# Attention and softplus MLP in split fp32: fewer round trips of the weights through DRAM, a new order of instructions

## The chip, the cores and the metric

The kernel runs on one core of a Trainium2 chip. The metric is the device time of one execution in microseconds, the median of several runs. The engines are TensorE (PE, matmuls; PEld is its weight load), VectorE (DVE), ScalarE (ACT), GpSimd (POOL, hardly used here) and SyncE (SP), which in this kernel issues the DMA transfers.

## The reference

A batch of attention with 32 states per head, 8 batches, 8 heads, 512 tokens, head width 64, is read in both directions, and the rows of both reads go through one MLP with a softplus:

```python
scores = scale * x @ state.T;  a = softmax(scores);   xread = a @ state
scores2 = scale * state @ x.T; a2 = softmax(scores2); sread = a2 @ x
y = concatenate([xread, sread])     # 8 x (512 + 32) rows per head
rows = y.transpose(0, 2, 1, 3).reshape(4352, 512)
out = softplus(rows @ w_in) @ w_out    # 512 -> 2048 -> 512
```

All inputs and the output are fp32 in value.

## The kernel before

**Arithmetic.** TensorE works in fp32r. A value is held as a high part, cast to fp32r, and a low part, the rest. ScalarE makes the high part (`copy`, L302), VectorE the low part by a subtraction (L318); the helper `split` (L314) makes both. A product then takes three passes (high by high, high by low, low by high). Each of the sixteen 128-row tiles of w_out is so split into a tile `W` of 128x1024 words, 512 KB; w_in is kept as eight 512 KB tiles `wf` of two 512-wide halves, and each half is split into a tile `u`, sixteen of 512 KB.

**Stages.** Batches 0 and 1, then 2, go through `gemm2` (L605): hidden tile `h`, softplus `t` (L589), split into `g`, and `acc` sums `W` times `g` over the sixteen tiles. From batch 3 on, pairs of hidden tiles and pairs of w_out tiles are multiplied in a form with seven products of half size (L762; the first half of batch 3 still plain, L772). The forms of w_out that this needs are made by VectorE and ScalarE between batch 2 and batch 3 from tiles `Wc`: sums `ci` (L690), the differences `cf` (L696 to L699), and their splits `T`, `E`, `W` (names F, E and Wc in the trace). The rows of the second read, `sread`, come from all batches and are calculated as an extra batch "8" between batches 6 and 7; their w_in tiles are `uu`. A read of states is `R` in the plan (`rp` in the trace); it takes the turned softmax weights `aT`, which go from VectorE's transposes to DRAM (`te`) and back in pieces. K products (`vq`, from `u` and `K`) make the folded weights `vt` of batches 4 to 7, stored as `vd` and loaded as `V`.

**What goes through DRAM.** Each `W` is stored once (`Sw`, `wd<-W`) and loaded again as `Wb` (tiles 8 to 15, for batch 2) and as `Wc` (all sixteen, for batch 3 and later, `Lc`). Each `u` is stored (`Su`, `ud<-u`) and loaded at the sread rows as `uu` (`Lu`).

**Order.** A text `PLAN` at the head of the kernel lists all some 2,580 steps, each with its engine (T is TensorE, A ScalarE, V VectorE, S SP; a few conversions of the inputs have letters of their own) and the buffers its results take. Every engine runs its steps in the order of that text, and SP issues the transfers in that order too, each after what it reads is there and the buffer it writes is free. A buffer comes free with the last reader of what it held. So the text sets both the order and what can collide.

Of the kernel before, what the change touches and what calls it, by code (L numbers as in the profile page):

```python
# [8 lines left out]
F32 = mybir.dt.float32  # L9
# [9 lines left out]
P = 128  # L19
# [18 lines left out]
PAIRS = ("w8", "o8", "x", "xT", "po", "wf", "W", "V", "a", "g", "u", "K", "vt", "gA", "gS", "F", "ev", "uu", "Wb", "Wc", "E")  # L38
# [73 lines left out]
Sv.2.1.0:S: m.2.11.2:T: s.2.15:A:13 Sv.2.1.1:S: m.2.11.3:T: gh.2.15:A:31 B.K3.0+K3.1:T:7,2,0,4 ci1.0:V:12 uh.3.3:A:6 uh.3.2:A:39 ul.3.3:V: m.2.12.0:T:
gh.v3.0.0:A:20 ul.3.2:V: Su.3.3:S: gh.v3.0.1:A:24 m.2.12.1:T: gl.v3.0.0:V: Su.3.2:S: gh.v3.1.0:A:22 m.2.12.2:T: gl.v3.0.1:V: gh.v3.1.1:A:15
# [172 lines left out]
def graph(io, at, nc):  # L286
# [10 lines left out]
    def r(ap):  # L297
        return ap.bitcast(F32R)
# [295 lines left out]
    def which(f, b):  # L594
        return "W" if b < 2 or b == 2 and f < 8 else "Wb" if b == 2 else "Wc"
# [354 lines left out]
```

## Time and profile before

| | |
|---|---|
| median of 3 runs | 655.26 us (653.18 to 655.49) |
| the profiled execution | 654.07 us, of which the span from first to last instruction 651.9 |
| mean granted TensorE clock | 0.987 |
| busy: TensorE, VectorE, ScalarE | 622.6, 460.7, 369.1 us |
| moved by DMA | 124.25 MB, HBM read 76.81 and written 46.66 |

TensorE is the busiest engine. Where a row shows a time in brackets, that is how long the engine stood before the group of instructions, and what it then got. A DMA row on SP is the time of issuing; the data lands later.

### The profile page before, as it was taken

Reading aid. Unit: us, or ns where it says so; the run is one execution under the profiler, and the core shown is the slowest. Engines: PE = TensorE matmul, PEld = TensorE weight load, DVE = VectorE, ACT = ScalarE, POOL = GpSimd, SP = SyncE. Lnnn points to the kernel's source line nnn. Section 1 sums busy time; section 2 is a strip of 40 time slices with the busy share of each in tenths; the row PEclk is TensorE's granted clock in tenths of the full one; section 3 lists DMA queues with packets and bytes.
Section 4 is the critical chain, followed back from the end, with each engine's and each line's share of the span. In section 5 each row is a group of like instructions: output and inputs, shape, how many; then the busy total and the mean of one; then the engine's idle time right before and its main releaser. Section 6 shows DMA issues by size and latency. Waiting matters only on the chain.

```text
span 651.9 us, 11867 instructions
## 1 busy us (share of the span) xinstructions
PE 622.6 (95%) x4398; PEld 527.6 (81%) x4398; DVE 460.7 (71%) x1005; ACT 369.1 (57%) x743; POOL 1.0 (0%) x7
## 2 busy tenths in 40 slices
PE   8999999999839999989799999999999999999997
PEld 6678787776626787768688999989899999999997
DVE  4998595647715586859988698479874666745493
ACT  4989684754806575556545664376563435445540
POOL 0000000000000000000000000000000000000000
PEclk9999999999959999999899999999999999999999
DMA  8952332303987999998665143547358124723000
GB/s 340 418 194 98 116 122 76 120 33 109 387 347 319 382 355 395 417 417 294 191 199 131 50 136 108 184 137 214 98 185 275 59 98 163 227 76 87 1 33 33
DMA packets 49113, 124.25 MB, mean 191 GB/s; under 512 B 6816, under 2 KB 16544, under 8 KB 49056
## 3 DMA queue, kind: packets, MB, share of 16 engines
q1 hardware_dynamic: 48912, 122.97, 53.8%
q8 instruction: 35, 0.57, 0.4%
q10 hardware_dynamic: 144, 0.52, 0.2%
q14 instruction: 22, 0.18, 0.1%
HBM read 76.81 MB, written 46.66 MB: 189 GB/s over the span
## 4 chain that ended last, share of the span: by engine, by line
PE 77%; DVE 10%; DMA 7%; SPq 3%; issue 1%; ACT 1%; DVEq 0%; ACTq 0%
PE h L321 25%; PE acc L321 19%; PE pk_X L762 8%; PE pk_Z L762 7%; PE pk_Y L762 7%; PE pk_Q L762 4%; PE vp L321 2%; SPq L312 2%; PE vq L321 2%; DMA aT<-te 2%; DMA wd<-W 2%; DVE gA L318 1%; DMA Wc<-wd 1%; DMA out_dram<-o 1%; PE sc L321 1%
## 5 line engine op out<-in xcount | busy, mean ns | idle before, releaser
L321 PE MATMUL h<-a,V 128*128 128x512 f32 x744 | 180.7, 391 | 2.4 <-ACT t L734 2.4
L321 PEld LDWEIGHTS h<-a,V 128*128 128x128 f32 x744 | 137.4, 188 | 31.2 <-ACT t L734 2.8
L321 PE MATMUL acc<-W,g 128*128 128x512 f32 x480 | 118.8, 397 | 0.0
L321 PEld LDWEIGHTS acc<-W,g 128*128 128x128 f32 x480 | 89.7, 189 | 26.1 <-issue 6.3
L734 ACT ACTIVATE t<-h 128x256 f32<-128x256 f32 x152 | 50.2, 384 | 67.5 <-PE h L321 55.5
L302 ACT CAST gS<-sf 128x512 fp32r<-128x512 f32 x73 | 45.1, 622 | 42.9 <-DVE sf L746 13.6
L318 DVE TENSOR_TENSOR gA<-t,gA 128x384 fp32r<-128x384 f32 (+1 forms) x76 | 42.4, 560 | 28.8 <-ACT gA L302 28.5
L318 DVE TENSOR_TENSOR gS<-sf,gS 128x512 fp32r<-128x512 f32 x73 | 49.4, 682 | 9.8 <-ACT gS L302 7.6
L302 ACT CAST gA<-t 128x384 fp32r<-128x384 f32 (+1 forms) x76 | 39.0, 521 | 23.6 <-PE pk_Q L762 9.3
L762 PE MATMUL pk_X<-Wc,gA 128*128 128x256 f32 x240 | 43.3, 288 | 3.1 <-DVE rs L481 1.6
L744 DVE TENSOR_TENSOR sf<-t 128x256 f32<-128x256 f32 x66 | 27.5, 417 | 24.3 <-ACT t L734 24.2
L318 DVE TENSOR_TENSOR g<-t,g 128x512 fp32r<-128x512 f32 x48 | 32.2, 684 | 15.7 <-ACT g L302 15.7
L762 PEld LDWEIGHTS pk_X<-Wc,gA 128*128 128x128 f32 x240 | 36.8, 191 | 6.7 <-DVE gA L318 3.7
L762 PE MATMUL pk_Z<-Wc,gS 128*128 128x256 f32 x240 | 41.8, 283 | 0.0
L762 PE MATMUL pk_Z<-Wc,gA 128*128 128x256 f32 x240 | 41.8, 283 | 0.0
L762 PE MATMUL pk_Y<-F,gS 128*128 128x256 f32 x240 | 41.8, 283 | 0.0
L762 PE MATMUL pk_Y<-Wc,gS 128*128 128x256 f32 x240 | 41.8, 283 | 0.0
L762 PE MATMUL pk_Q<-E,gA 128*128 128x256 f32 x240 | 41.8, 283 | 0.0
L762 PE MATMUL pk_X<-F,gS 128*128 128x256 f32 x240 | 41.8, 283 | 0.0
L589 ACT ACTIVATE t<-h 128x512 f32<-128x512 f32 x48 | 27.7, 600 | 24.6 <-PE h L321 23.4
L762 PEld LDWEIGHTS pk_Z<-Wc,gA 128*128 128x128 f32 x240 | 34.6, 192 | 0.0
L762 PEld LDWEIGHTS pk_Q<-E,gA 128*128 128x128 f32 x240 | 34.6, 192 | 0.0
(167 smaller groups left out, 973.7 us busy)
## 6 DMA issues: line engine op xcount, KB each, us to landing
vd<-vt SPq DMA_DIRECT2D x32, 512.0 KB, 7.5
V<-vd SPq DMA_DIRECT2D x128, 128.0 KB, 3.1
w<-in_w_in_dram SPq DMA_DIRECT2D x16, 512.0 KB, 8.2
o<-in_w_out_dram SPq DMA_DIRECT2D x16, 512.0 KB, 9.8
x<-in_xn_dram SPq DMA_DIRECT2D x16, 512.0 KB, 4.8
wd<-W SPq DMA_DIRECT2D x16, 512.0 KB, 9.6
ud<-u SPq DMA_DIRECT2D x16, 512.0 KB, 6.4
Wc<-wd SPq DMA_DIRECT2D x16, 512.0 KB, 10.3
```

The costliest lines, as they stand in the source:

```text
L302: nc.scalar.copy(dst, src)
L312: op(name, "S", ins, list(outs), lambda e: nc.sync.dma_start(dst(), src()))
L318: lambda e: eng(e).tensor_tensor(r(dlo()), src(), dhi(), ALU.subtract))
L321: nc.tensor.matmul(dst, lhs, rhs, start=start, stop=stop)
L589: lambda e: nc.scalar.activation(at(f"t.{k}"), at(f"h.{k}"), AF.Softplus))
L734: nc.scalar.activation(dst, src.rearrange("p (c t) -> p c t", t=P), AF.Softplus)
L744: nc.vector.tensor_tensor(o[:, 0:2], a[:, 0:3:2], a[:, 3:4].broadcast_to([P, 2, P]), ALU.subtract)
L762: nc.tensor.matmul(at(bank)[:, 256 * half:256 * half + 256], r(g[:, gi, P * blk:P * blk + P]), r(wform(u, m)(wi)), start=first and pi == p ...
```

## The change

Three things are changed in the code.

- **W.** Only tiles 8 to 15 are stored (`Sw`), earlier and each near where its split is finished; they are loaded as `Wb` for batch 2 as before and as `Wc` for batch 3 and later. Tiles 0 to 7 keep their place on chip to the end: batch 3 and later read `W.0` to `W.7` in place of `Wc.0` to `Wc.7` (`which`, `wt`).
- **w_in for the sread rows.** The sixteen stores of `u` and loads of `uu` are replaced by eight stores of the unsplit `wf` (`Sf`, `fd<-wf`) and eight loads (`Lf`, into `wg`). `wg` is split anew by sixteen casts `xh` on ScalarE and sixteen subtractions `xl` on VectorE into `uu`.
- **A new `PLAN`** from there on: same matmuls, another order on all engines and other buffers.

```diff
+AWAY, BACK = (8, 9, 10, 11, 12, 13, 14, 15), (8, 9, 10, 11, 12, 13, 14, 15)
 PLAN = """
...
-Lx.1.0:S:0 Lx.1.1:S:2 qk.2.1:A:6 Sw.13:S: h.2.0:T:6 A.3.0:V:0 Sw.11:S: qk.3.1:A:2 Sw.10:S: qk.3.0:A:10 vl.2.1.0:V: Sw.1:S: o.0.2.2:V: Sw.9:S:
+tl.0:V: m.1.15.3:T: m.1.13.1:T: o.1.1.3:V: m.1.14.1:T: Ms.2.0:V: Sw.15:S: Sw.13:S: Sw.14:S: So.1.3:S: m.1.15.1:T: Se.1.0:S: m.1.12.2:T: o.1.1.1:V:
...
     def which(f, b):
-        return "W" if b < 2 or b == 2 and f < 8 else "Wb" if b == 2 else "Wc"
+        return "Wc" if b > 2 and f in BACK else "Wb" if b >= 2 and f in AWAY else "W"
 
-    for f in range(NFT):
+    for f in sorted({*AWAY, *BACK}):
         store(f"Sw.{f}", [f"W.{f}:h", f"W.{f}:l"], lambda f=f: io.wd[f], lambda f=f: at(f"W.{f}"), [f"D:wd.{f}"])
-        for w in ("Wb", "Wc")[f < 8:]:
+        for w in ["Wb"] * (f in AWAY) + ["Wc"] * (f in BACK):
             load(f"L{w[1]}.{f}", [f"{w}.{f}:h", f"{w}.{f}:l"], lambda f=f, w=w: at(f"{w}.{f}"), lambda f=f: io.wd[f], [f"D:wd.{f}"])
...
     for c in range(4):
+        for i in range(2):
+            whole = [W1[0, j, i] for j in range(2)] if c == 0 else [W1[c, 2 * i + q] for q in range(2)]
+            store(f"Sf.{c}.{i}", whole, lambda c=c, i=i: io.fd[c, i], lambda c=c, i=i: at(f"wf.{c}.{i}"), [f"D:fd.{c}.{i}"])
+            load(f"Lf.{c}.{i}", [f"wg.{c}.{i}:"], lambda c=c, i=i: at(f"wg.{c}.{i}"), lambda c=c, i=i: io.fd[c, i], [f"D:fd.{c}.{i}"])
         for q in range(4):
...
-            store(f"Su.{k}", [f"u.{k}:h", f"u.{k}:l"], lambda k=k: io.ud[k], lambda k=k: at(f"u.{k}"), [f"D:ud.{k}"])
-            load(f"Lu.{k}", [f"uu.{k}:"], lambda k=k: at(f"uu.{k}"), lambda k=k: io.ud[k], [f"D:ud.{k}"])
+            split(f"xh.{k}", f"xl.{k}", lambda c=c, q=q: page(f"wg.{c}.{q // 2}", 2, 512)[:, q % 2],
+                  lambda k=k: page(f"uu.{k}", 2, 512)[:, 0], lambda k=k: page(f"uu.{k}", 2, 512)[:, 1], [f"wg.{c}.{q // 2}:"], f"uu.{k}:h", f"uu.{k}:l", "A")
...
-            op(f"ci{i}.{u}", "V", [f"Wc.{f}:h", f"Wc.{f}:l"], [f"{buf}:0"],
+            op(f"ci{i}.{u}", "V", [f"{wt(f, 3)}:h", f"{wt(f, 3)}:l"], [f"{buf}:0"],
...
-            op(f"h.8.{u}.{i}", "T", [f"uu.{u // 2}.{kt}:" for kt in range(4)] + [f"sreadT:{x}{b}" for b in range(B) for x in "hl"],
+            op(f"h.8.{u}.{i}", "T", [f"uu.{u // 2}.{kt}:{x}" for kt in range(4) for x in "hl"] + [f"sreadT:{x}{b}" for b in range(B) for x in "hl"],
```

The same replacement of `Wc` by `wt(f, 3)` stands in the splits and products of the later batches. Three places of the new order follow.

SP, at the start of batch 2, before. `wd<-W` is a store `Sw`, `aT<-te` a piece of the turned softmax weights of the read of batch 1, x the rows it reads; the sixteen stores begin right after x.

```order
L309 DMA x_0_1718<-in_xn_dram 128x1024
L309 DMA x_1_1720<-in_xn_dram 128x1024
L312 DMA wd_111<-W_1444 128x1024
L312 DMA wd_109<-W_1079 128x1024
...
L312 DMA wd_102<-W_664 128x1024
L312 DMA out_dram<-po_1_498 128x512
L312 DMA te_70<-tr_0_1794 128x512
L309 DMA aT_0_1586<-te_68 32x4x128 x3
L312 DMA te_71<-tr_1_1815 128x512
L312 DMA te_73<-tr_1_1828 128x512
L309 DMA ks<-in_stk_dram 64x4x128
```

The same place of SP in the changed kernel:

```order
L313 DMA out_dram<-po_0_500 128x512
L310 DMA x_0_1726<-in_xn_dram 128x1024
L310 DMA x_1_1728<-in_xn_dram 128x1024
L310 DMA ks<-in_stk_dram 64x4x128 x2
L310 DMA aT_0_1594<-te_68 32x4x128 x3
L313 DMA te_70<-tr_0_1777 128x512
L313 DMA te_71<-tr_1_1779 128x512
L313 DMA out_dram<-po_1_490 128x512
L313 DMA out_dram<-po_0_500 128x512
L313 DMA te_73<-tr_1_1835 128x512
```

The pieces of `aT` stand behind x and ks, and no store of W is left there: seven of the eight stand before batch 1's outputs, one further ahead.

TensorE, around the read of batch 1, before. `vp` is a product for the folded weights of batch 3, `rp` the read, `acc` the sums of batch 2 with the hidden tile `g_1`, the second of the batch.

```order
L321 MATMUL vp_3_1_1866<-wf_1_1090,zf_1254 32x512
L321 MATMUL rp_1867<-x_0_1718,aT_0_1586 32x64 x2
L321 MATMUL rp_1867<-x_1_1720,aT_0_1586 32x64 x2
...
L321 MATMUL rp_1867<-x_1_1720,aT_1_1096 32x64 x2
L321 MATMUL acc_0_0_1838<-W_305,g_1_1818 128x512 x3
L321 MATMUL acc_0_1_1843<-W_305,g_1_1818 128x512 x3
L321 MATMUL h_5_1936<-a_0_1608,V_1_0_1707 128x512 x3
```

And in the changed kernel, where `vq` are the K products and `g_4` is the fifth hidden tile of batch 2:

```order
L322 MATMUL vq_1_1_1986<-u_1_1931,K 128x512
L322 MATMUL acc_0_0_1824<-W_656,g_4_1901 128x512 x3
L322 MATMUL acc_0_1_1829<-W_656,g_4_1901 128x512 x3
L322 MATMUL acc_0_2_1839<-W_656,g_4_1901 128x512 x3
L322 MATMUL acc_0_3_1845<-W_656,g_4_1901 128x512 x3
L322 MATMUL vp_3_0_2027<-wf_0_1074,zf_1255 32x512
...
L322 MATMUL rp_2029<-x_0_1726,aT_0_1594 32x64 x2
L322 MATMUL rp_2029<-x_1_1728,aT_0_1594 32x64 x2
```

The read has moved from before the sums of the second hidden tile to after those of the fifth, and three K products stand ahead of it.

ScalarE, at the sread rows, before. `gS` and `gA` are the splits for the products of batch 6's second half, `t` the softplus of the sread rows.

```order
L302 CAST gS_1_4_5956<-arena_5720 128x512
L302 CAST gA_1_4_5960<-t_1_4_5585 128x384
L302 CAST gS_1_5_5996<-sf_1_5_5916 128x512
L734 ACTIVATE t_0_0_6012<-h_0_5983 128x2x128
L734 ACTIVATE t_0_0_6012<-h_0_5983 128x256
L302 CAST gA_1_5_6054<-t_1_5_5609 128x384
L302 CAST gS_1_6_6056<-sf_1_6_5976 128x512
```

And in the changed kernel, with `wg` the loaded tile and `uu` its split; `T` is a table of exponentials:

```order
L303 CAST gS_1_6_5985<-sf_1_6_5952 128x512
L303 CAST gA_1_7_6001<-t_1_7_5697 128x384
L303 CAST uu_0_6004<-wg_0_5925 128x512
L303 CAST uu_1_6019<-wg_0_5925 128x512
L739 ACTIVATE t_0_0_6022<-h_0_5987 128x2x128
L446 ACT_TABLE_LOAD
L446 ACTIVATE T_0_4943<-T_0_4943 128x512
L303 CAST uu_2_6039<-wg_1_5927 128x512
```

The casts `xh` of the second group stand between the splits of the products and the softplus of the sread rows.

## Rows read from the trace of the kernel before

**Rows 1.** The page: busy time of the engines; DMA share in forty slices.
```profile
PE 622.6 (95%) x4398; PEld 527.6 (81%) x4398; DVE 460.7 (71%) x1005; ACT 369.1 (57%) x743; POOL 1.0 (0%) x7
...
DMA  8952332303987999998665143547358124723000
```
**Rows 2.** Waits of TensorE: line, released by, us in total, times, longest.
```profile
PE rp L321 <- DMA aT<-te: 13.7, 1, 13.7
PE pk_Z L772 <- ACT gA L302: 2.4, 1, 2.4
PE h L321 <- ACT t L734: 2.4, 1, 2.4
PE pk_X L762 <- DVE rs L481: 1.6, 1, 1.6
PE pk_X L762 <- DVE gA L318: 1.5, 1, 1.5
PE pk_Z L772 <- DVE gA L318: 1.4, 2, 0.9
```
**Rows 3.** Timeline of SP's queue, 155 to 190: start, us, engine, operation, count.
```profile
161.53 17.36 SPq L312 DMA_DIRECT2D wd<-W  x16
...
182.05 2.79 SPq L309 DMA_DIRECT2D aT<-te  x3
```
**Rows 4.** Timeline of TensorE, 190 to 201 us.
```profile
190.46 1.94 PE L321 MATMUL rp<-x,aT 128*32 128x64 f32 x64 [13.69 <-DMA aT<-te]
192.33 2.67 PE L321 MATMUL acc<-W,g 128*128 128x512 f32 x6
...
196.21 1.52 PE L321 MATMUL acc<-W,g 128*128 128x512 f32 x6
197.66 1.66 PE L321 MATMUL vq<-u,K 64*128 64x512 f32 x12
```
**Rows 5.** Windows: length, busy PE, PEld, DVE, ACT, POOL; granted clock, DMA share, GB/s.
```profile
176.00:194.60 18.60, 4.91 (x86) 3.55 (x71) 4.52 (x9) 3.51 (x7) 0.00 (x0) 0.63 0.96 375
...
317.70:321.20 3.50, 3.50 (x13) 2.90 (x12) 3.36 (x10) 1.62 (x3) 0.00 (x0) 0.55 0.31 93
```
**Rows 6.** Timeline of TensorE, 276 to 340 us.
```profile
317.72 2.76 PE L772 MATMUL pk_Q<-Wc,gA 128*128 128x512 f32 x6
...
323.61 1.20 PE L321 MATMUL rp<-x,arena 128*32 128x64 f32 x64
```
**Rows 7.** Timeline of ScalarE, 270 to 290 us.
```profile
270.54 2.09 ACT L302 CAST vt<-vq 128x512 fp32r<-128x512 f32 x4
...
283.15 0.38 ACT L734 ACTIVATE t<-h 128x256 f32<-128x256 f32 x1 [9.69 <-DMA out_dram<-o]
```
**Rows 8.** Timeline of VectorE, 274 to 292 us.
```profile
284.42 1.29 DVE L690 TENSOR_TENSOR c<-Wc 128x512 f32<-128x512 f32 x2 [7.59 <-DMA out_dram<-o]
...
288.07 0.68 DVE L690 TENSOR_TENSOR arena<-Wc 128x512 f32<-128x512 f32 x1
288.67 0.69 DVE L318 TENSOR_TENSOR F<-c,F 128x512 fp32r<-128x512 f32 x1
```
**Rows 9.** Windows around 250 to 300 us and at the sread rows.
```profile
250.00:290.00 40.00, 37.14 (x198) 27.41 (x197) 26.18 (x49) 20.31 (x48) 0.00 (x0) 1.00 1.03 418
290.00:300.00 10.00, 10.00 (x46) 8.29 (x45) 9.72 (x21) 6.45 (x19) 0.00 (x0) 1.00 0.98 379
...
540.00:550.00 10.00, 10.00 (x86) 10.00 (x85) 4.36 (x10) 4.92 (x10) 0.00 (x0) 1.00 0.63 211
```
**Rows 10.** The page: a cast and a subtraction of 128x512; count, busy us, mean ns.
```profile
L302 ACT CAST gS<-sf 128x512 fp32r<-128x512 f32 x73 | 45.1, 622 | 42.9 <-DVE sf L746 13.6
...
L318 DVE TENSOR_TENSOR gS<-sf,gS 128x512 fp32r<-128x512 f32 x73 | 49.4, 682 | 9.8 <-ACT gS L302 7.6
```
**Rows 11.** Issues of 512 KB loads, page and 520 to 580 us: median to landing.
```profile
Wc<-wd SPq DMA_DIRECT2D x16, 512.0 KB, 10.3
...
uu<-ud SPq DMA_DIRECT2D x9, 512.0 KB, 3.7
```

More of the change, by code (lines that the diff above doesn't have):

```diff
@@ L251 @@
[L251 to L253 removed]
+Lx.1.0:S:0 Lx.1.1:S:2 vh.2.3.0:A:9 Lk.0:S:6 h.2.0:T:6 E.2.0:V: Lk.1:S: qk.2.1:A:0 Le.1.0.0:S: qk.3.0:A:2 E.2.1:V: Le.1.0.1:S: e.2.0:A: Le.1.0.2:S:
@@ new lines @@
+h.3.0:T:7 A.4.0:V:6 vh.3.2.0:A:10 Lc.15:S:15 vh.3.2.1:A:22 A.4.1:V:10 qk.4.0:A:1 vl.3.2.0:V: h.3.1:T:3 qk.4.1:A:5 E.4.0:V: s.3.0.0.0:A:67
+s.3.1.0.0:A:68 E.4.1:V: Le.2.0.0:S:77 h.3.2:T:4 s.3.0.0.1:A: Le.2.0.1:S: s.3.1.0.1:A: vl.3.2.1:V: Le.2.0.2:S: Le.2.0.3:S: h.3.3:T:2 gh.3.0.0:A:3
+Le.2.1.0:S:78 gl.3.0.0:V: Le.2.1.1:S: Le.2.1.2:S: h.3.4:T:6 s.3.0.1.0:A:67 Le.2.1.3:S: s.3.1.1.0:A:15 s.3.0.1.1:A: Le.3.0.0:S:16 s.3.1.1.1:A:
+Le.3.0.1:S: gh.3.0.1:A:5 h.3.5:T:0 Le.3.0.2:S: s.3.0.2.0:A:95 gl.3.0.1:V: Le.3.0.3:S: s.3.1.2.0:A:96 Le.3.1.0:S:91 p.3.0.0.0:T:1 s.3.0.2.1:A:
@@ new lines @@
+sf.4.1.2:V:6 p.4.0.7.2:T: e2.4.0:V: p.4.0.7.3:T: e3.4.0:V: p.4.1.0.0:T:3 Sh.4.1.1:A:0 e4.4.0:V: e5.4.0:V: gh.4.1.4:A:33 p.4.1.0.1:T:7 Sl.4.1.1:V:
+So.4.0.0:S: p.4.1.0.2:T:1 e6.4.0:V: p.4.1.0.3:T:5 sf.4.1.3:V:11 So.4.0.1:S: p.4.1.1.0:T: Sh.4.1.2:A:16 gl.4.1.3:V: p.4.1.1.1:T: Sl.4.1.2:V:
+p.4.1.1.2:T: sf.4.1.4:V:14 p.4.1.1.3:T: Sh.4.1.3:A:20 gl.4.1.4:V: p.4.1.2.0:T: r.5.0:V: gh.4.1.5:A:0 Sl.4.1.3:V: p.4.1.2.1:T: sf.4.1.5:V:2
+p.4.1.2.2:T: gl.4.1.5:V: p.4.1.2.3:T: Sh.4.1.4:A:22 r.5.1:V: p.4.1.3.0:T: Lv.5.1.0.0:S:40 Sl.4.1.4:V: Lv.5.1.0.1:S: p.4.1.3.1:T: sf.4.1.6:V:13
@@ new lines @@
+sf.5.0.1:V:10 p.4.1.6.1:T: gh.5.0.0:A:34 gl.5.0.0:V: p.4.1.6.2:T: p.4.1.6.3:T: p.4.1.7.0:T: Sh.5.0.0:A:20 gh.5.0.1:A:32 p.4.1.7.1:T: Sl.5.0.0:V:
+p.4.1.7.2:T: gl.5.0.1:V: p.4.1.7.3:T: h.5.4:T:4 e1.4.1:A:0 Sh.5.0.1:A:33 e2.4.1:V: e3.4.1:V: h.5.5:T:6 s.5.0.2.0:A:14 e4.4.1:V: s.5.1.2.0:A:2
+e5.4.1:V: e6.4.1:V: So.4.1.0:S: p.5.0.0.0:T:0 Sl.5.0.1:V: s.5.0.2.1:A: So.4.1.1:S: s.5.1.2.1:A: p.5.0.0.1:T:2 sf.5.0.2:V:13 p.5.0.0.2:T:3
+p.5.0.0.3:T:7 B.Q6+R5:T:4,1,5 Sh.5.0.2:A:20 gh.5.0.2:A:34 Sl.5.0.2:V: gl.5.0.2:V: p.5.0.1.0:T: X.5:V:8 qk.6.0:A:5 Lv.5.2.0.0:S:16 A.6.0:V:0
@@ new lines @@
+h.7.7:T:0 gl.7.0.2:V: s.7.0.3.0:A:10 s.7.1.3.0:A:2 p.7.0.1.0:T: s.7.0.3.1:A: s.7.1.3.1:A: sf.7.0.3:V:9 p.7.0.1.1:T: gh.7.0.3:A:0 gl.7.0.3:V:
+p.7.0.1.2:T: p.7.0.1.3:T: Sh.7.0.3:A:2 h.7.8:T:3 Sl.7.0.3:V: h.7.9:T:6 s.7.0.4.0:A:6 s.7.1.4.0:A:8 p.7.0.2.0:T: s.7.0.4.1:A: s.7.1.4.1:A:
+sf.7.0.4:V:12 p.7.0.2.1:T: gh.7.0.4:A:10 gl.7.0.4:V: p.7.0.2.2:T: p.7.0.2.3:T: Sh.7.0.4:A:16 h.7.10:T:2 Sl.7.0.4:V: h.7.11:T:0 s.7.0.5.0:A:1
+s.7.1.5.0:A:13 p.7.0.3.0:T: s.7.0.5.1:A: s.7.1.5.1:A: sf.7.0.5:V:4 p.7.0.3.1:T: gh.7.0.5:A:34 gl.7.0.5:V: p.7.0.3.2:T: p.7.0.3.3:T: Sh.7.0.5:A:23
@@ new lines @@
+h.7.12:T:3 Sl.7.0.5:V: h.7.13:T:6 s.7.0.6.0:A:3 s.7.1.6.0:A:7 p.7.0.4.0:T: s.7.0.6.1:A: s.7.1.6.1:A: sf.7.0.6:V:0 p.7.0.4.1:T: gh.7.0.6:A:37
+gl.7.0.6:V: p.7.0.4.2:T: p.7.0.4.3:T: Sh.7.0.6:A:22 h.7.14:T:2 Sl.7.0.6:V: h.7.15:T:0 s.7.0.7.0:A:10 s.7.1.7.0:A:9 p.7.0.5.0:T: s.7.0.7.1:A:
+gh.7.0.7:A:26 sf.7.0.7:V:6 p.7.0.5.1:T: s.7.1.7.1:A: gh.7.1.0:A:0 gl.7.0.7:V: p.7.0.5.2:T: gh.7.1.1:A:2 sf.7.1.0:V:12 p.7.0.5.3:T: Sh.7.0.7:A:10
+p.7.0.6.0:T: gl.7.1.0:V: gh.7.1.2:A:16 Sl.7.0.7:V: p.7.0.6.1:T: sf.7.1.1:V:1 p.7.0.6.2:T: gl.7.1.1:V: p.7.0.6.3:T: Sh.7.1.0:A:20 gl.7.1.2:V:
@@ L254 @@
+Sl.7.1.4:V: p.7.1.3.1:T: sf.7.1.6:V:5 p.7.1.3.2:T: gl.7.1.7:V: p.7.1.3.3:T: Sh.7.1.5:A:17 p.7.1.4.0:T: Sl.7.1.5:V: p.7.1.4.1:T: sf.7.1.7:V:6
+p.7.1.4.2:T: p.7.1.4.3:T: Sh.7.1.6:A:13 p.7.1.5.0:T: Sl.7.1.6:V: p.7.1.5.1:T: p.7.1.5.2:T: p.7.1.5.3:T: Sh.7.1.7:A:0 p.7.1.6.0:T: Sl.7.1.7:V:
+p.7.1.6.1:T: p.7.1.6.2:T: p.7.1.6.3:T: p.7.1.7.0:T: p.7.1.7.1:T: e1.7.1:A:20 e2.7.1:V: p.7.1.7.2:T: e3.7.1:V: p.7.1.7.3:T: e4.7.1:V: e5.7.1:V:
+e6.7.1:V: So.7.1.0:S: So.7.1.1:S:
 """
@@ L688, in graph @@
         for i, (f, buf) in enumerate(((f1, c1), (f2, c2))):
-            op(f"ci{i}.{u}", "V", [f"Wc.{f}:h", f"Wc.{f}:l"], [f"{buf}:0"],
-               lambda e, f=f, buf=buf: nc.vector.tensor_tensor(at(buf), page(f"Wc.{f}", 2, DM)[:, 0], page(f"Wc.{f}", 2, DM)[:, 1], ALU.add))
+            op(f"ci{i}.{u}", "V", [f"{wt(f, 3)}:h", f"{wt(f, 3)}:l"], [f"{buf}:0"],
+               lambda e, f=f, buf=buf: nc.vector.tensor_tensor(at(buf), page(wt(f, 3), 2, DM)[:, 0], page(wt(f, 3), 2, DM)[:, 1], ALU.add))
         def forms(e, c1=c1, c2=c2, c3=c3):
@@ L705, in graph @@
               [f"{c2}:1"], f"E.{u // 2}:h{u}", f"E.{u // 2}:l{u}", "A")
-        split(f"Wh.{u}", f"Wl.{u}", lambda c1=c1: at(c1)[:, 256:512], lambda f1=f1: page(f"Wc.{f1}", 2, DM)[:, 0, 256:512],
-              lambda f1=f1: page(f"Wc.{f1}", 2, DM)[:, 1, 256:512], [f"{c1}:1"], f"Wc.{f1}:Th", f"Wc.{f1}:Tl", "A")
+        split(f"Wh.{u}", f"Wl.{u}", lambda c1=c1: at(c1)[:, 256:512], lambda f1=f1: page(wt(f1, 3), 2, DM)[:, 0, 256:512],
+              lambda f1=f1: page(wt(f1, 3), 2, DM)[:, 1, 256:512], [f"{c1}:1"], f"{wt(f1, 3)}:Th", f"{wt(f1, 3)}:Tl", "A")
     def wform(u, n):
         lo, hi = slice(0, 256), slice(256, 512)
-        return {"B11": lambda x: page(f"Wc.{2 * u}", 2, DM)[:, x, lo], "T1": lambda x: page(f"Wc.{2 * u}", 2, DM)[:, x, hi],
-                "B21": lambda x: page(f"Wc.{2 * u + 1}", 2, DM)[:, x, lo], "B22": lambda x: page(f"Wc.{2 * u + 1}", 2, DM)[:, x, hi],
+        return {"B11": lambda x: page(wt(2 * u, 3), 2, DM)[:, x, lo], "T1": lambda x: page(wt(2 * u, 3), 2, DM)[:, x, hi],
+                "B21": lambda x: page(wt(2 * u + 1, 3), 2, DM)[:, x, lo], "B22": lambda x: page(wt(2 * u + 1, 3), 2, DM)[:, x, hi],
                 "T2": lambda x: page(f"F.{u}", 2, 512)[:, x, lo], "T3": lambda x: page(f"F.{u}", 2, 512)[:, x, hi],
@@ L771, in direct @@
                             for x, (gi, wi) in enumerate(PASSES):
-                                nc.tensor.matmul(at(bank), r(page(f"gA.{k}", 2, 512)[:, gi, P * blks[i]:P * blks[i] + P]), r(page(f"Wc.{2 * u + i}", 2, DM)[:, wi]),
+                                nc.tensor.matmul(at(bank), r(page(f"gA.{k}", 2, 512)[:, gi, P * blks[i]:P * blks[i] + P]), r(page(wt(2 * u + i, 3), 2, DM)[:, wi]),
                                                  start=first and i + x == 0, stop=x == 2, skip_group_check=True)
-                    op(f"p.{k}.{j}", "T", [f"gA.{k}:h", f"gA.{k}:l"] + [f"Wc.{2 * u + i}:{x}" for i in range(2) for x in "hl"] + ([f"{bank}:{opened[bank]}"] if bank in opened else []),
+                    op(f"p.{k}.{j}", "T", [f"gA.{k}:h", f"gA.{k}:l"] + [f"{wt(2 * u + i, 3)}:{x}" for i in range(2) for x in "hl"] + ([f"{bank}:{opened[bank]}"] if bank in opened else []),
                        [f"{bank}:{u}"], direct)
@@ L837, in attention_then_softplus_mlp @@
     io.te = {f"{b}.{g}": dp.tile([P, S], F32, tag=f"te{b}{g}", name=f"te{b}{g}") for b in MOVED for g in range(2)}
-    io.ud = {f"{c}.{q}": dp.tile([P, 1024], F32, tag=f"ud{c}{q}", name=f"ud{c}{q}") for c in range(4) for q in range(4)}
+    io.fd = {(c, i): dp.tile([P, 1024], F32, tag=f"fd{c}{i}", name=f"fd{c}{i}") for c in range(4) for i in range(2)}
     io.wd = [dp.tile([P, 1024], F32, tag=f"wd{f}", name=f"wd{f}") for f in range(NFT)]
```

349 lines of the change are left out of this document (162 added, 187 removed).

## The prediction

> **What bounds the kernel now.** I read the page's table of busy time first. TensorE is busy for 622.6 us, 95% of the span, VectorE for 460.7, ScalarE for 369.1 [rows 1]. The change leaves the matmuls as they are, so the reader should look for what the other 5% are: TensorE's idle time, and beside it the time in which its clock is low. The waits of TensorE are the second view [rows 2]. One wait, of rp for the DMA aT<-te, is 13.7 us, more than half of all; the next five are 2.4, 2.4, 1.6, 1.5 and 1.4.
>
> Third, the timeline of the DMA queue ahead of that wait [rows 3]. SP issues sixteen stores wd<-W in a row from 161.53, and they hold it for 17.36 us, 1.1 us each. Only then, at 182.05, does it issue the last three pieces of aT, for which TensorE stands from 176.8 to 190.46 [rows 4]. The data of aT was not late, its turn in SP's queue was. When the matmuls return they run at the half clock: the mean over 176 to 194.6 us is 0.63 [rows 5], with 64 rp matmuls in 1.94 us, where 64 at full clock take 1.20 [rows 6], and 6 acc in 2.67 where the next 6 of that shape take 1.52 [rows 4]. That is 0.74 + 1.15 = 1.9 us.
>
> Fourth, the stretch from batch 2 into batch 3. ScalarE sits idle for 9.69 us until 283.15 and VectorE for 7.59 us until 284.42, both for the stores out_dram<-o [rows 7, 8]: their results are to be written where the outputs still wait to leave, and from 250 to 290 us the DMA engines move 418 GB/s at a share of 1.03 [rows 9]. Afterwards VectorE is busy 9.72 of 10 us [rows 9], and TensorE pays with 2.4 (h<-ACT t), 2.4 (pk_Z<-ACT gA), 1.4 (pk_Z<-DVE gA) and 1.6 (pk_X<-DVE rs) [rows 2], about 7.75 us, and with a clock of 0.55 from 317.7 to 321.2 [rows 5]: 6 pk_Q in 2.76 us instead of 1.52 [rows 6], 1.24 us lost.
>
> **The stores of W.** Eight of the sixteen go, and the other eight leave earlier, each where its tile is made. The last three pieces of aT then stand right behind the loads of x and ks in SP's order, as the order of the change shows, so they are issued near 163 us. The slowest kind of transfer here, Wc under load, takes 10.3 us to land [rows 11]; even so aT would be there by 174, before TensorE asks for it at 176.8. Besides, the order puts rp behind the accumulations of batch 2's tiles 1 to 4 and three K products, some 15 us of matmuls. Either half alone would remove the wait; I take −13.7 and −1.9 for the clock. What is late next there is the softplus and split chain of h.2.x, and the K products, whose results must be cast and split before the next K finds its banks free: the first bank is full some 0.8 us in (12 matmuls in 1.66 [rows 4]), four casts take 2.09 [rows 7], a last subtract 0.68 and the handovers the rest, 4.0 us by estimate, against 1.66 for the product and 2.9 for the 12 acc matmuls behind it (6 in 1.52, less overlap). It fits with half a microsecond to spare; I charge nothing.
>
> At the clock a page of the Trainium skill speaks too (TensorE: Matmul & The Clock Gate, section Terms): the penalty is the throttled time times the share of clock withheld. With 0.63 over 18.6 us about 13.8 us were throttled, so by it some 6.9 us would come back, not 1.9, and the time would fall to 629 us, that of the second rival. Most of that throttled time is the wait itself, already counted, and the matmul rows show what is left; the rows decide, and the rule adds nothing to that rival's chance.
>
> **The transfers that vanish.** 8 stores and 8 loads of W, 8 stores and 8 loads of the split u, 32 × 512 KB = 16.8 MB. The eight new stores of fp32 w_in lie before 115 us, in slices where the DMA share is 2 or 3 tenths [rows 1] and SP waits; I cost them at nothing (if that cover were gone, each holds SP for 1.1 us as the wd stores did, 8.8 in all). From the stretch between 190 and 300 us go the 16 stores of u and the 8 loads Wc, 12.6 MB or 30 us of DMA at 418 GB/s, and the out stores no longer queue behind a backlog. So the idle 7.59 and 9.69 us on VectorE and ScalarE go, but TensorE's gain is only what was passed on to it: the 7.75 and 1.24 above.
>
> Not all of it. VectorE stays the tighter engine there: one 128x512 operation starts every 0.60 us (288.07, 288.67 [rows 8]), and the forms of W cost it the same as before, only earlier. Walking the new VectorE order at such pitches beside the matmuls, it is behind in four places: at K2.2 0.85 us, at the reads of batches 2 and 3 1.2, at two products of the second half 0.1 and 0.45; 2.6 us come back. Bounds: 0 (the earlier forms give all the slack that is needed) and 9 (all as before). I stay near the lower end because the 7.59 us of idle VectorE are almost exactly the 7.75 that TensorE lost.
>
> **New casts and subtracts.** 16 casts xh at 622 ns are 10.0 us of ScalarE, 16 subtracts xl at 682 ns 10.9 us of VectorE [rows 10]. In the stretch of the sread rows they lie beside TensorE, which is busy 10 of 10 us from 540 to 550 while VectorE is busy for 4.36 and ScalarE for 4.92 [rows 9]: covered, with about 0.7 us to spare at the tightest place (the last tile of the third group, whose slot is freed by the matmuls just ahead). Without that cover each group of four would cost up to 0.62 + 0.68 = 1.3 us. ScalarE takes its work in order: in [rows 7] one t waits 9.69 us for a DMA, and nothing of ScalarE runs meanwhile. So an xh whose tile has not landed also stops the gA and gS casts behind it. That is the fourth rival.
>
> **The order of the later batches.** Hidden matmuls now run two pairs ahead of the products instead of three, so less is in stock when a batch's half ends and VectorE has to do the six ends too. By the same walk TensorE waits some 0.5 us at four of the half boundaries of batches 4 to 7: +2.0, bounds 0 and 5. Against it stands the pk_X wait of 1.5 us at 460.8, which sits at an old order's place and goes: −1.5.
>
> **Sum.** The profiled execution took 654.07 us (span 651.9). 654.07 − 13.7 − 1.9 − 7.75 − 1.24 + 2.6 + 2.0 − 1.5 = 632.6. It lies 1.2 us under the median of the runs, 655.26; the forecast for the median is 633.8, say 634.
>
> **Rivals.** First, only SP's wait goes. The stretch at 280 to 340 us stays bound by VectorE: all 9 us are lost again because the forms, splits and row sums there are the same work. For it speaks 9.72 of 10 us, which is work and not waiting; against it that VectorE stood for 7.59 us just before. 634 + 9 − 2.6 = 640.4, say 640.
>
> Second, no new waits anywhere: 654.07 − 13.7 − 1.9 − 9.0 − 1.5 + 1.2 = 629. For it speaks that VectorE is busy 71% and its order was made anew; against, that the lead in hidden tiles is shorter.
>
> Third, the change does not do what it says: SP is held by something else (a te<-tr whose source is late, a vd store) and aT is again late by as much. For it speaks that SP issues strictly one after another [rows 3]; against, that in the new order nothing with a late source stands before aT. About 654, no change.
>
> Fourth, and slower: the fp32 tiles of w_in arrive late at the sread rows. Three of the four groups can be loaded only when a slot is free. On the nearly idle queue the uu loads landed in 3.7 us (median), under load Wc loads took 10.3 [rows 11]. If the loads find the queue full, each group is 6.6 us late, ScalarE stands before its xh with the gS casts of the products behind it, and each such wait costs a low clock like the 1.9 above: 3 × (6.6 + 1.9) = 25.5, so 659.5. It decides, against the half per cent below, from 6.3 us of lateness per group. Against it: TensorE never waited there, the loads are now half as many bytes, and the share of DMA in 540 to 550 is 0.63 [rows 9].
>
> **How the numbers follow.** Chances: forecast 0.62 (its own range 630.5 to 638), first rival 0.16, second 0.15, third 0.03, fourth 0.04. Half a per cent is 3.3 us, about what a measurement of this kernel can tell from no change. Faster by more: the forecast and the first two, 0.93; within: 0.03; slower: 0.04. The range runs from 627.5, a little under the second rival, to 644, which holds the first with an unhidden boundary or two; what lies beyond is the third, the fourth and an error of my walk.
>
> **What would show it.** In the changed profile rp's wait for aT is gone, the granted clock stays at 1.0 (2.4 GHz) past 190 us, and aT is issued before 170. The idle times of VectorE and ScalarE for out_dram<-o near 260 to 270 us are under 2 us. TensorE's waits sum to under 11 us, the longest of them in batch 3 and on VectorE's gA, gS or vt. At the sread rows no wait for wg is longer than 1 us. I am wrong if TensorE has one wait over 4 us, if the batch 2 to 3 stretch loses 7 us or more (first rival), or if uu<-wg is what TensorE or ScalarE waits for (fourth).

## The result and the profile after

The changed kernel takes 629.88 us (median of 4 runs, 629.45 to 630.39) against 655.26; the ratio is 0.962, 95% interval 0.9599 to 0.9641, 25 us less. The forecast was 634 with a range of 627.5 to 644. The profiled execution took 630.39, its span 628.2 us, and its mean granted clock 1.0.

The page of the changed kernel, busy time [rows 1]:

```profile
PE 619.2 (99%) x4398; PEld 525.6 (84%) x4398; DVE 470.4 (75%) x1018; ACT 380.8 (61%) x762; POOL 1.0 (0%) x7
```

As many matmuls as before, but 3.4 us less busy time; the prediction's matmul rows had put the cost of the low clock at 3.1. VectorE has 9.7 us more and ScalarE 11.7, about the new splits. All waits of TensorE in the changed kernel [rows 2]:

```profile
PE rp L322 <- DVE vt L319: 1.1, 1, 1.1
PE h_idle L882 <- DVE idle L880: 1.1, 1, 1.1
PE vq L322 <- DVE u L319: 0.7, 1, 0.7
PE sc L322 <- DMA zf<-in_zp_dram: 0.5, 1, 0.5
PE pk_X L767 <- DVE gS L319: 0.3, 1, 0.3
PE sc L322 <- ACT g L303: 0.3, 1, 0.3
PE st L416 <- ACT e L303: 0.2, 1, 0.2
```

They sum to 4.2 us. The 1.1 of h_idle, before the work starts, is among them, as it was before the change. SP's queue at the start of batch 2 in the changed kernel [rows 3], then TensorE [rows 4], then the window [rows 5]:

```profile
161.19 0.81 SPq L310 DMA_DIRECT2D x<-in_xn_dram  x2
162.10 1.30 SPq L310 DMA_DIRECT2D ks<-in_stk_dram  x2
163.45 1.55 SPq L310 DMA_DIRECT2D aT<-te  x3
168.04 0.93 SPq L313 DMA_DIRECT2D te<-tr  x2
169.21 3.32 SPq L313 DMA_DIRECT2D out_dram<-po  x2
```

```profile
187.95 1.66 PE L322 MATMUL vq<-u,K 64*128 64x512 f32 x12
189.54 3.01 PE L322 MATMUL acc<-W,g 128*128 128x512 f32 x12
192.49 1.09 PE L322 MATMUL vp<-wf,zf 64*32 64x512 f32 x16
193.51 1.10 PE L322 MATMUL rp<-x,aT 128*32 128x64 f32 x64
```

```profile
176.00:194.60 18.60, 18.60 (x167) 12.96 (x165) 12.41 (x20) 11.78 (x24) 0.00 (x0) 1.00 0.68 255
```

aT is issued at 163.45 instead of 182.05, and rp, which asks for it at 193.51, waits for nothing. TensorE works through the whole window, at full clock.

Something less expected stands in the DMA view of the changed kernel from 230 to 270 us, its issues of the out stores of batch 2 (KB each, median us to landing):

```profile
out_dram<-o SPq DMA_DIRECT2D x4, 256.0 KB, 8.4
```

They land as late as before, where the same view of 250 to 290 us gave 8.4 too. But no compute engine waits for them now: the idle 9.69 us of ScalarE and 7.59 us of VectorE [rows 7, 8] have no counterpart. SP issues them earlier; first its row in the kernel before, then the first such row of the changed kernel:

```profile
273.74 4.01 SPq L312 DMA_DIRECT2D out_dram<-o  x4
```

```profile
248.01 0.34 SPq L313 DMA_DIRECT2D out_dram<-o  x1
```

One more line is wanted later, TensorE's only wait near the sread rows in the changed kernel:

```profile
506.14 0.39 PE L767 MATMUL pk_X<-F,gS 128*128 128x256 f32 x1 [0.35 <-DVE gS L319]
```

### The profile page after: what moved, and what is told of

Same layout as the page of the kernel before. It is cut to its first block, busy times and chain, and to the rows that moved or that the text cites. A ratio compares the mean times of both kernels' runs of the same rounds, so it can differ in the third digit from the quotient of the medians.

```text
span 628.2 us, 11843 instructions
## 1 busy us (share of the span) xinstructions
PE 619.2 (99%) x4398; PEld 525.6 (84%) x4398; DVE 470.4 (75%) x1018; ACT 380.8 (61%) x762; POOL 1.0 (0%) x7
## 4 chain that ended last, share of the span: by engine, by line
PE 86%; DVE 10%; issue 1%; DMA 1%; ACT 1%; DVEq 0%; SPq 0%; ACTq 0%
PE h L322 29%; PE acc L322 21%; PE pk_X L767 8%; PE pk_Z L767 8%; PE pk_Y L767 8%; PE pk_Q L767 4%; PE vp L322 2%; PE vq L322 2%; DVE gA L319 1%; PE sc L322 1%; DVE gS L319 1%; PE rp L322 1%; DMA zf<-in_zp_dram 1%; DVE sf L749 1%; PE ss L322 1%
## 5 line engine op out<-in xcount | busy, mean ns | idle before, releaser
L322 PE MATMUL h<-a,V 128*128 128x512 f32 x744 | 178.5, 391 | 0.0
L322 PE MATMUL acc<-W,g 128*128 128x512 f32 x480 | 116.6, 394 | 0.0
L322 PEld LDWEIGHTS acc<-W,g 128*128 128x128 f32 x480 | 89.1, 188 | 24.8 <-issue 5.3
L303 ACT CAST gS<-sf 128x512 fp32r<-128x512 f32 x76 | 47.2, 621 | 64.5 <-DVE sf L751 29.4
L319 DVE TENSOR_TENSOR gS<-sf,gS 128x512 fp32r<-128x512 f32 x76 | 51.9, 683 | 14.7 <-ACT gS L303 14.3
L767 PEld LDWEIGHTS pk_X<-F,gS 128*128 128x128 f32 x240 | 35.0, 191 | 1.7 <-DVE gS L319 1.5
L767 PEld LDWEIGHTS pk_Y<-F,gS 128*128 128x128 f32 x240 | 34.5, 192 | 0.0
L303 ACT CAST g<-t 128x512 fp32r<-128x512 f32 x48 | 29.2, 623 | 1.3 <-PE acc L322 0.5
L303 ACT CAST V<-vp 128x512 fp32r<-128x512 f32 x30 | 16.2, 593 | 18.1 <-PE vp L322 17.9
L319 DVE TENSOR_TENSOR vt<-vq,vt 128x512 fp32r<-128x512 f32 x32 | 20.0, 681 | 7.5 <-ACT vt L303 7.4
L322 PE MATMUL h<-sreadT,uu 128*128 128x256 f32 x192 | 24.1, 282 | 0.0
```

The costliest lines, as they stand in the source:

```text
L303: nc.scalar.copy(dst, src)
L319: lambda e: eng(e).tensor_tensor(r(dlo()), src(), dhi(), ALU.subtract))
L322: nc.tensor.matmul(dst, lhs, rhs, start=start, stop=stop)
L767: nc.tensor.matmul(at(bank)[:, 256 * half:256 * half + 256], r(g[:, gi, P * blk:P * blk + P]), r(wform(u, m)(wi)), start=first and pi == p ...
```

## The experiments

Each ran on the same chip as runs of the kernel before, and the ratio is to those. The theory: the sixteen stores of W in a row made the first stall, by keeping SP from what stands behind them; the second loss came from transfers that kept the out stores from leaving. The rivals: the place of the read rp alone, and the new order as such.

**Moving aT ahead.** Kernel before; in the plan, three steps change place:

```diff
-... Sw.4:S: ... So.0.2:S: ... Se.2.0:S: ... Le.1.0.2:S: ... Le.1.0.0:S: ... Le.1.0.1:S:
+Lx.1.1:S:2 Le.1.0.2:S: Le.1.0.0:S: Le.1.0.1:S: ... Sw.13:S: ...
```

> The kernel before, with only the last three pieces of aT moved ahead of the sixteen stores of W in SP's order. If the wait of rp was the whole stall, the time falls by 13.7 plus 1.9 for the clock, to about 639.5. My theory: SP's queue made the stall, and ks, which the K products need, stands behind the same stores, so the wait moves to K: ks lands near 190, is cast and split, K starts near 192 where it could start near 183; TensorE loses about 9 us there and some clock, and the time falls by 4 to 6 only, to 649 to 652. If the data of aT and not its turn was late: no change, 655.

653.22 us, ratio 0.9979 (0.9962 to 0.9995). The largest wait of TensorE in this run, and the instruction of ScalarE that made it:

```profile
PE vq L321 <- ACT K L302: 10.6, 1, 10.6
```

```profile
191.72 0.62 ACT L302 CAST K<-ks 128x512 fp32r<-128x512 f32 x1 [13.10 <-DMA ks<-in_stk_dram]
```

The wait of rp is gone, 13.7 us of it, and 10.6 come back at K, for ks, a load that stands behind the same stores. The gain was 1.4 us, less than my 4 to 6: K waited longer than the 9 us I had put, and the low clock came back (that vq takes 2.93 us instead of 1.66).

**Moving aT and ks ahead.** As before, with `Lk.0:S:4 Lk.1:S:` also moved behind `Lx.1.1`.

> The kernel before, with the three pieces of aT and both loads of ks ahead of the sixteen stores. Theory (SP's turn): no wait of rp and none of K over 1 us, clock at 1.0 through 200 us, time down by 13.7 + 1.9 to 638 to 641; the stretch from 276 to 340 us loses its 9 us as before. Rival (the stores hold the DMA engines, whoever is issued first, and what follows is late too, as the stores of u and vd): TensorE waits again within 30 us, time above 645.

654.15 us, ratio 0.9998 (0.9988 to 1.0008): no gain that can be measured. Waits of TensorE, SP's queue, and two instructions of ScalarE in this run:

```profile
PE h L321 <- DVE vt L318: 9.5, 1, 9.5
...
PE vq L321 <- ACT K L302: 2.8, 1, 2.8
```

```profile
161.38 1.38 SPq L309 DMA_DIRECT2D aT<-te  x3
170.15 1.30 SPq L309 DMA_DIRECT2D ks<-in_stk_dram  x2
171.49 18.05 SPq L312 DMA_DIRECT2D wd<-W  x16
```

```profile
176.43 0.62 ACT L302 CAST g<-t 128x512 fp32r<-128x512 f32 x1 [1.24 <-DMA wd<-W]
...
195.81 0.62 ACT L302 CAST g<-t 128x512 fp32r<-128x512 f32 x1 [6.28 <-DMA out_dram<-po]
```

Three things went wrong for the theory as I had put it. ks needs a buffer that comes free only at 170, so SP stood there and the stores began 9 us later. And ScalarE waits for wd<-W itself: the casts g of batch 2 write where tiles of W lay, and those come free when their stores have landed. The longest wait, the 9.5 us of h, goes back through vt to a g that writes where an output lay, whose store stood behind the burst (the 6.28 us). So the burst holds engines in two ways, by SP's turn and by slots. The run is no clean test of the turn.

**The burst put back into the changed kernel.** All sixteen `Sw` in the old sequence behind `Lx.1.1`, those of tiles 8 to 15 taken from their early places; the second of the two runs also has both loads of ks ahead of the stores:

```diff
-    for f in sorted({*AWAY, *BACK}):
+    for f in range(NFT):
```

```diff
-Lx.1.1:S:2 ... Lk.0:S:6 ... Lk.1:S: ... Le.1.0.0:S:
+Lx.1.1:S:2 Sw.13:S: Sw.11:S: ... Sw.4:S: ... Lk.0:S:6 ... Lk.1:S: ... Le.1.0.0:S:
```

> The changed kernel, with all sixteen stores of W (those of tiles 0 to 7 are read by nothing) in one row behind x, ahead of ks and aT, and none earlier. My prediction said that either half alone removes the wait of rp: then rp at 193.5 does not wait for aT, which lands near 190. But ks stands behind the burst too: it lands near 187 to 190, and the first K product, now at 178.9, waits about 11 us: 641 to 646. If the place of rp is all that counts: 630. If rp waits all the same: its row shows aT.

> As the run before, but with both loads of ks ahead of the sixteen stores and aT behind them. Theory: K is on time, aT lands near 190, rp asks at 193.5, nothing is lost: 629.5 to 631.5, although SP is held for 17 us as before. Rival: the 8 MB of stores in a row make te, vd or Wb late and TensorE waits elsewhere by 3 us or more: 633 and up.

648.66 us, ratio 0.9914 (0.9899 to 0.9929), and 649.56, ratio 0.993 (0.9915 to 0.9945): some 19 us of the 25 are lost, with ks ahead or not. TensorE's largest wait in the first of them, then in the second, and there ScalarE's:

```profile
PE h L322 <- ACT e L502: 16.1, 1, 16.1
```

```profile
PE h L322 <- ACT e L502: 17.2, 1, 17.2
```

```profile
182.09 0.58 ACT L303 CAST V<-vp 128x512 fp32r<-128x512 f32 x1 [20.92 <-DMA wd<-W]
```

Neither aT nor ks: a cast V writes where a tile of W lies whose store has just been moved late, and everything behind it on ScalarE stands for 20.92 us (19.85 in the first of the two runs). Both expectations missed this; the rival of the second had the size, 633 and up, but named te, vd or Wb. In the new order the early stores are not only out of SP's way, they free slots that the order counts on.

**SP's turn without slots.** Changed kernel; sixteen stores that nothing reads and that free nothing, between ks and aT:

```diff
+    for f in range(16):
+        store(f"Sx.{f}", [f"W.{f % 8}:h", f"W.{f % 8}:l"], lambda f=f: io.wx[f], lambda f=f: at(f"W.{f % 8}"))
```

> The changed kernel with sixteen stores of tiles W.0 to W.7 (each twice, read by nothing, freeing no slot) between ks and aT: SP is held for some 17 us, but no tile waits for a store. Theory: aT is issued near 181, lands near 190, rp asks at 193.5 and does not wait, ks is there: 629.5 to 632. This separates SP's turn from the slots, which made the two runs with the burst put back lose 19 us. Rival: SP's turn alone costs, through te, vd or Wb behind it: 635 or more.

641.33 us, ratio 0.9786 (0.9768 to 0.9805), 11 us slower than the change. The largest wait of TensorE, SP's queue, and ScalarE:

```profile
PE vq L323 <- DVE vt L320: 8.6, 1, 8.6
```

```profile
162.80 17.74 SPq L314 DMA_DIRECT2D wx<-W  x16
180.59 3.21 SPq L311 DMA_DIRECT2D aT<-te  x3
183.90 1.43 SPq L314 DMA_DIRECT2D te<-tr  x2
186.22 1.59 SPq L314 DMA_DIRECT2D out_dram<-po  x2
```

```profile
191.26 0.58 ACT L304 CAST vt<-vq 128x512 fp32r<-128x512 f32 x1 [10.45 <-DMA out_dram<-po]
```

rp did not wait for aT, as expected, but the out stores behind aT went at 186.22 instead of 169.21, and vt writes where their data lay. How long these two took to land, in this run (180 to 195 us), then in the changed kernel (163 to 178 us):

```profile
out_dram<-po SPq DMA_DIRECT2D x2, 256.0 KB, 4.6
```

```profile
out_dram<-po SPq DMA_DIRECT2D x2, 256.0 KB, 2.0
```

So 15 to 17 us of their delay are their turn in SP's order (the second went at 187.5 instead of 172.2), and 2.6 are a slower landing. A hold of 17.7 us costs some 11 with no slot in the burst itself; with rp moved away, the next in the queue takes the wait. The rival was right in size; it named te, vd or Wb, and it was the out stores.

**The same dead stores from GpSimd.** `store` replaced by a transfer that GpSimd issues.

> As the run before with the sixteen dead stores, but GpSimd issues them, which does nothing else: the DMA engines carry the same 8.4 MB, SP is free. If SP's turn made the stall (aT, po and te stand behind the stores in its order): 629.5 to 632. If the DMA engines' time made it (an out store issued behind 8.4 MB lands late, whoever issues): vt waits for out_dram<-po as before, 637 or more.

629.37 us, ratio 0.9612 (0.9593 to 0.963), as fast as the change. But GpSimd, with nothing else to do, issued them as soon as the tiles were there (ns shortest, median, longest; first and last start):

```profile
L603 POOL DMA_DIRECT2D wx<-W x16: 533/533/1468, 23.6 to 61.8; - x16
```

So the run shows that 8.4 MB more, issued before 62 us, cost nothing. It does not test the cover of the early stores of W, which go later, from 100 to 136 us; for that speaks only that TensorE waits 0.3 us in all from 100 to 200 us in the changed kernel. Nor does it show whether a transfer that another engine issues in the middle of the burst would land in time; that stays open.

**The burst taken out of the old order.** Kernel before; `Sw.8` to `Sw.15` at the early places of the change, `Sw.0` to `Sw.7` left out.

```diff
-        store(f"Sw.{f}", ...
+        if f >= 8:
+            store(f"Sw.{f}", ...
-            load(f"L{w[1]}.{f}", ..., lambda f=f: io.wd[f], ...
+            load(f"L{w[1]}.{f}", ..., lambda f=f: io.wd[f if f >= 8 else f + 8], ...
```

> The kernel before in its old order, with the burst gone: stores of W.8 to W.15 placed early as in the change, stores of W.0 to W.7 left out (the loads Wc of these tiles read the stored tiles 8 to 15 instead, so the transfers stay and the values of batch 3 and later differ). Theory: the burst made the stall twice over, by SP's turn (aT, ks) and by the slots that its tiles free only when their stores have landed; without it rp, K and g wait for nothing and the time falls by the 13.7 + 1.9 of the prediction to 638 to 641, with the losses from 276 to 340 us as before. Rival: in the old order the next thing is late (the wait moves again, as it did in the two runs before): above 645.

638.81 us beside 655.48 on this chip, ratio 0.9753 (0.9731 to 0.9775), 16.7 us less; 638 to 641 was expected. Its waits begin with the losses of the second stretch:

```profile
PE h L321 <- ACT t L735: 3.0, 1, 3.0
PE pk_X L763 <- DVE gA L318: 2.6, 3, 1.5
PE pk_Z L773 <- ACT gA L302: 1.7, 1, 1.7
PE pk_X L763 <- DVE rs L481: 1.7, 1, 1.7
```

**The stores of u taken out of the old order.**

```diff
-            store(f"Su.{k}", ...
-            load(f"Lu.{k}", ..., lambda k=k: io.ud[k], ...
+            load(f"Lu.{k}", ..., lambda c=c, q=q: io.wd[8 + (4 * c + q) % 8], ...
```

> The kernel before in its old order, without the sixteen stores of the split u (8.4 MB less from 190 to 270 us; the loads of uu read stored W tiles instead, so the rows of the second read differ). The stall at 176 to 190 stays in both theories. Backlog theory: the out stores of batch 2 land in 2 to 4 us instead of 8.4, VectorE's idle 7.59 falls under 2, and TensorE loses 5 to 9 us less from 284 to 340: 646 to 650. Order theory (the forms simply stand too late in the old order): 653 to 656.

646.66 us beside the same 655.48, ratio 0.9868 (0.9849 to 0.9888), 8.8 us less, in the range of the backlog theory; 1.2 us of it lie in the first stall, where rp waits 12.5 instead of 13.7. The first waits, and the out stores from 250 to 290 us:

```profile
PE rp L320 <- DMA te<-tr: 12.5, 1, 12.5
PE pk_X L760 <- DVE gA L317: 2.5, 4, 1.5
```

```profile
out_dram<-o SPq DMA_DIRECT2D x4, 256.0 KB, 5.6
```

h<-ACT t and pk_Z<-gA are gone, pk_X<-rs stays. The out stores landed in 5.6 us rather than 2 to 4, but were issued 5 us earlier (268.41, not 273.74), since SP had no stores of u to issue.

**Both.** The two edits together:

> Both edits of the two runs before at once, still the old order: what the removed transfers alone are worth. If the two gains add up: 630 to 634, and the new order is worth 0 to 4 us beyond them. If the new order carries the second half of the gain: 638 to 641.

630.64 us, ratio 0.9628 (0.9611 to 0.9646). The gains add up (16.7 + 8.8 against 24.8), and the old order without these stores is as fast as the changed kernel within the intervals, though it still loads all sixteen `Wc`. It is no substitute, since it leaves out stores whose data the later batches need. Its waits:

```profile
PE pk_X L760 <- DVE gA L316: 3.0, 3, 1.5
PE pk_X L760 <- DVE rs L479: 1.7, 1, 1.7
```

**The stores of u put back into the new order.**

```diff
+            store(f"Su.{k}", [f"u.{k}:h", f"u.{k}:l"], lambda k=k: io.ud[k], lambda k=k: at(f"u.{k}"), [f"D:ud.{k}"])
```

> The changed kernel with the sixteen stores of the split u back in SP's order, right behind their split, read by nothing. In the old order these 8.4 MB were worth 8.8 us. If the new order only made room for the edits and the transfers carry the gain: the out stores land late again, VectorE and TensorE lose 4 to 9 us: 634 to 639. If the earlier forms in the new order cover the backlog by themselves: 629.5 to 631.5.

629.95 us, ratio 0.962 (0.9604 to 0.9637): nothing lost. In its view of 230 to 270 us the out stores land as slowly as ever, and no compute engine waits for them:

```profile
out_dram<-o SPq DMA_DIRECT2D x4, 256.0 KB, 8.3
```

So for the second loss either is enough: the old order without u's stores, or the new order with them. Eight of the loads `Wc` are still gone here; the new order with these as well was not run.

**The new splits doubled.**

```diff
     def split(hi, lo, src, dhi, dlo, ins, ohi, olo, engines="AG"):
+        n = 2 if hi.startswith("xh.") else 1
-        op(hi, engines, ins, [ohi], lambda e: copy(e, r(dhi()), src()))
+        op(hi, engines, ins, [ohi], lambda e: [copy(e, r(dhi()), src()) for _ in range(n)])
```

and the same for the subtraction.

> The changed kernel with every cast xh and every subtraction xl of the sread rows done twice: 10.0 us more on ScalarE, 10.9 on VectorE. From 490 to 550 VectorE has 60 less 52.5, about 7.5 us, free in the changed kernel. If the new splits are covered with what room there is: the second 10.9 do not fit, TensorE loses some 3 us and some clock, 632 to 636. If they are covered amply, as I predicted (VectorE at half load there): under 631.

639.66 us, ratio 0.9765 (0.9745 to 0.9785), 10 us slower than the change, more than either expectation and about what was added on either engine. New waits of TensorE; then the window of 490 to 550 us in this run and in the changed kernel:

```profile
PE h L323 <- DVE uu L320: 2.3, 3, 1.3
PE pk_X L768 <- DVE gS L320: 2.1, 2, 1.8
PE h L323 <- ACT uu L303: 1.4, 1, 1.4
```

```profile
490.00:550.00 60.00, 55.15 (x427) 54.05 (x426) 54.95 (x118) 37.84 (x74) 0.00 (x0) 0.94 0.25 80
```

```profile
490.00:550.00 60.00, 59.65 (x499) 59.41 (x498) 52.55 (x119) 34.74 (x71) 0.00 (x0) 1.00 0.29 97
```

VectorE has 7.5 us free in the changed kernel, not the half that I had read from one window of before, and the order uses it tightly. TensorE's waits sum to 9.3 us, 5.1 more than in the change, and its busy time is 4.4 us more (623.6 against 619.2) at the clock of 0.94 here: together they are the ten.

**K2.2+K2.3 and R2+R3 each one product later.**

```diff
-B.K2.2+K2.3:T:4,2,1,7 ... p.3.1.1.0:T: ... B.R2+R3:T:4,2 ... p.3.1.2.0:T:
+p.3.1.1.0:T: B.K2.2+K2.3:T:4,2,1,7 ... p.3.1.2.0:T: B.R2+R3:T:4,2
```

> The changed kernel with the products K2.2+K2.3 one product later and the reads R2+R3 one product later, at the two places where TensorE still waits (0.7 and 1.1 us). If these are handovers that a little lead removes: 1 to 1.8 us less, 628 to 629. If VectorE is the bound there (9.7 of 10 us busy), the waits move to the next products: within 0.5 us of 629.9.

632.23 us, ratio 0.9651 (0.9631 to 0.967), some 2 us slower. The wait, and the K product behind it:

```profile
PE pk_X L767 <- ACT gS L303: 2.0, 1, 2.0
```

```profile
300.94 2.93 PE L322 MATMUL vq<-u,K 64*128 64x512 f32 x12
```

The waits for vt and u are gone and a longer one for gS stands in their place. In all TensorE waits 4.7 us, hardly more than 4.2; what is lost is busy time, 621.3 us against 619.2, at a granted clock of 0.50 from 300.9 to 304 us (the K product in 2.93 us for 1.66). VectorE is the bound there, as the theory said: the cast gS had itself waited 1.75 us for VectorE's u. "Within 0.5 us" was too narrow.

## Why the prediction was right, and where not

**The first stall, −13.7 and −1.9.** Right in cause and size: taking the burst out of the old order gives 16.7 us against 15.6. What failed is half of the sentence that either half alone would remove the wait. The first half does: without the burst rp can stay at its old place. The second does not: with rp moved and a burst present rp waited for nothing, but others did, and the changed order lost 19, 19 and 11 us. Moving the victims ahead of the burst gained 1.4 us, and with ks 0.5, which cannot be told from nothing. I had looked at the one instruction that waited and at one way of being held; ks, the out stores and the slots of W stood behind the same stores.

**The clock.** The sum took 1.9 + 1.24 = 3.1 us from matmul rows; TensorE's busy time fell by 3.4. The rule of the Trainium skill (TensorE: Matmul & The Clock Gate, section Terms) would by estimate have given 6.9 for the first stretch alone; the trace does not agree with it there, where the matmul rows show 1.9 and 13.7 of the 18.6 us were idle.

**The second stretch, −7.75 and −1.24, +2.6.** The size was about right: the waits I had counted are gone in the changed kernel, and so are all but pk_X<-rs (1.7) in the old order without the stores of u. The walk was right at two places, 0.85 at K2.2 is 0.7 and 1.2 at R2+R3 is 1.1; the 0.55 at two products did not come. The reason was half right. I wrote that the out stores would no longer queue; in the changed kernel they land in 8.4 us as before, and nobody waits. They are issued at 248 instead of 274 us, but 15 of these 26 are the first stretch's, and going earlier alone does not help: in the run without the burst they went at 258.60, and VectorE and ScalarE still stood 8.3 and 10.4 us for them. In the new order no instruction waits for their slots.

**The half boundaries, +2.0.** Wrong: the changed kernel has no wait there; two pairs ahead are enough. No run tells why my walk was late, so that stays open. The 1.5 us of pk_X went, as forecast.

**The new splits, 0.** Nearly right as a result, wrong in its reason. TensorE waits for no uu, and nothing waits for wg. It waits 0.35 us at 506.14 for a subtraction gS that stands on VectorE behind two xl (from 504.20); with the splits doubled that wait is 1.81. The cover was not half a free engine, as the window of 540 to 550 us [rows 9] had me say; in the next one, 550 to 560, VectorE was busy 9.66 us even before the change. In the changed kernel the splits start at 492.9 us, where VectorE is nearly full. The doubled ones cost 10 us.

**The sum.** As measured, TensorE's waits fell from 24.7 us (the six of [rows 2] and 1.7 of small ones) to 4.2 and its busy time by 3.4: 654.07 − 20.5 − 3.4 = 630.2, beside 630.39 for the profiled execution. Of the 4.1 us between 634 and 629.88, two are the half boundaries and 1.7 come from the median: I had added 1.2 us for it, and this time it lies 0.5 below the profiled run. The time lies in the stated range but under 630.5, where I had put the lower end of the forecast's own: by the number alone the second rival, 629, to which I gave 0.15, was nearer. By the mechanism the waits at K2.2 and R2+R3 are the forecast's, and the half boundaries the rival's. The first rival (the second stretch loses as before) is excluded by the waits of 4.2 us; the third and fourth did not occur.

## What to carry to other kernels

When one long wait traces back to a burst in an in-order issue queue, count everything behind the burst and every slot that its tiles free, not only the instruction that waited last: with the burst there, moving the victims ahead gained at most 1.4 us of 15.6. A loss can have two sufficient cures, as the second stretch here; before crediting one, take each out alone and put each back alone. Read the cover of added work in the place where the new order puts it, and measure it by doubling that work.

## What the runs showed of the hardware that I had not expected

A 512 KB store took 1.0 to 1.1 us of SP's time while the DMA engines were full (16 in 16.23 to 18.08 us, in seven runs; DMA share 0.99 in the kernel before) and 0.32 us alone (wd<-W at 135.68 in the changed kernel); GpSimd's median issue of the same size was 0.53 us, before 62 us. A cast on ScalarE stood for 20.92 us for a store of the tile whose place it writes. A wait of TensorE can cost more than itself, and its length alone does not say when: behind the 2.0 us of the last run above, which 0.37 more followed, the granted clock was 0.50 and a K product took 2.93 us instead of 1.66, while behind the 2.35 us at 284.2 in the kernel before the granted clock was 1.00 (284 to 287 us) and twelve h matmuls took 3.04 us, against 2.88 for the next twelve.
